# Attention backward for one query: the stores of the last head but one, moved to chosen DMA engines

## The chip, the cores and the metric

The kernel runs on one core of one Trainium2 chip. The metric is the device time of one execution in microseconds (us), from the first to the last instruction; the kernel before has a median of 1286.99 us over three runs (1286.27 to 1288.67). The core has five instruction streams: TensorE (PE, with its weight load PEld), VectorE (DVE), ScalarE (ACT), GpSimd (POOL) and SyncE (SP). Data moves between HBM and SBUF through 16 DMA engines, which all queues share. GpSimd and SyncE each issue transfers to a queue of their own.

## The reference

The forward pass is attention with one query per head; the outputs are the result and the gradients of q, k and v.

```python
B, H, Sq, Sk, D = 2, 32, 1, 8192, 128          # bf16

def _fwd_reference(q, k, v):
    scale = q.shape[-1] ** -0.5
    scores = jnp.einsum("bhqd,bhkd->bhqk", q, k) * scale
    p = _softmax(scores, axis=-1)
    return jnp.einsum("bhqk,bhkd->bhqd", p, v)

def reference(q, k, v, grad_out):
    _out, _vjp = jax.vjp(_fwd_reference, q, k, v)
    return (_out, *_vjp(grad_out))             # out, dq, dk, dv
```

There are 64 heads. For each, K and V (2 MB each) are read and dK and dV (2 MB each) are written: dV is the outer product of p and grad_out, and dK that of the gradient of the scores and q. That makes 268 MB in and 268 MB out.

## The kernel before

A head's K or V is one tile of 128 partitions x 64 rows x 128 values; each partition holds 16 KB that are contiguous in HBM too. Heads are loaded six ahead, on SyncE. The scores come out of TensorE after transposes, and VectorE writes the outer products over the tile that held K or V (`outer`, four calls a tile), which is then stored.

```python
NTILE = 12
FIRST = 6
SPREAD = range(5, 64, 9)
...
    load_eng = nc.sync
    store_eng = nc.gpsimd
...
    def by_rows(eng, dst, src, rows):

        p = 0
        for m in rows:
            pin(eng.dma_start(out=dst[p : p + m], in_=src[p : p + m], max_dma_last_dim=NT * D))
            p += m
```

Just after the first load, six rows of q are read by GpSimd, after its cursor over the DMA engines has been set back; the other rows are read by SyncE:

```python
        r0 = FIRST if w == 0 else 0
        if r0:
            pin(store_eng.inc_swdge_sem([], [], mode="reset_dge_cursor"))
            pin(
                store_eng.dma_start(
                    out=qd_nat[:r0, w, :], in_=rows[:r0], max_dma_last_dim=D
                )
            )
        pin(load_eng.dma_start(out=qd_nat[r0:BH, w, :], in_=rows[r0:BH]))
```

How a store is issued, at the end of `outer` (w is 1 for dV and 0 for dK; `ends` is the list of chunks after which something is stored: the whole tile, or for the last head each of four chunks):

```python
        if c + 1 in ends:
            at = ends.index(c + 1)
            b0, b1 = (ends[at - 1] if at else 0) * CH, (c + 1) * CH
            dst = (dv_v if w else dk_v)[i]
            if w == 0 and i in SPREAD:
                by_rows(store_eng, dst, h.tile[w], (P - 2, 2))
            else:
                eng = load_eng if len(ends) > 1 else store_eng
                pin(eng.dma_start(out=dst[:, b0:b1, :], in_=h.tile[w][:, b0:b1, :]))
```

So all stores of heads 0 to 62 are GpSimd's, one transfer of 128 rows of 16 KB each; at every ninth head from the fifth (the last is head 59) dK goes as 126 rows and 2 rows. The eight chunks of head 63 (512 KB each) are SyncE's. After the loop two small outputs of 64 rows of 256 bytes follow on SyncE:

```python
    for w, (src, dst) in enumerate(((dqT, out_1), (oT, out_0))):
        ...
        load_eng.dma_start(out=dst.rearrange("b h s d -> (b h s) d"), in_=nat[:BH, 0, :])
```

Of the kernel before, what the change touches and what calls it, by code (L numbers as in the profile page):

```python
# [20 lines left out]
SPREAD = range(5, 64, 9)  # L21
# [3 lines left out]
def kernel(  # L25
# [12 lines left out]
    B, H, Sq, D = q.shape  # L38
    Sk = k.shape[2]
    P = nc.NUM_PARTITIONS  # L40
    assert Sq == 1 and D == P
    BH = B * H
    assert BH <= P
    NT = Sk // P
# [5 lines left out]
    load_eng = nc.sync  # L50
    store_eng = nc.gpsimd
    pin = tc.keep_in_program_order
# [30 lines left out]
    def by_rows(eng, dst, src, rows):  # L83

        p = 0
        for m in rows:
            pin(eng.dma_start(out=dst[p : p + m], in_=src[p : p + m], max_dma_last_dim=NT * D))
            p += m

    def load(i, w, pieces=(NCH,)):  # L90
        h = heads[i]
        t = kvp.tile([P, NT, D], BF16, tag=f"kv{slot_of(i, w)}", name="kvt")
        h.tile[w] = t
        src = (v_v if w else k_v)[i]
        c = 0
        for m in pieces:
            n0, n1 = c * CH, (c + m) * CH
            pin(load_eng.dma_start(out=t[:, n0:n1, :], in_=src[:, n0:n1, :]))  # L98
            c += m
# [4 lines left out]
    for w, a in enumerate((q, grad_out)):  # L104
        rows = a.rearrange("b h s d -> (b h s) d")
        r0 = FIRST if w == 0 else 0
        if r0:
# [3 lines left out]
                    out=qd_nat[:r0, w, :], in_=rows[:r0], max_dma_last_dim=D  # L111
# [276 lines left out]
    def outer(i, w, c, ends):  # L388

        h = heads[i]  # L390
        n0 = c * CH
        shape = [P, CH, D // 2, 2]
        pin(
            nc.vector.tensor_tensor(  # L394
                out=h.tile[w][:, n0 : n0 + CH, :].rearrange("p n (e t) -> p n e t", t=2),
                in0=h.qb[w][:]
                .rearrange("p (e t) -> p e t", t=2)
                .unsqueeze(1)
                .to_broadcast(shape),
                in1=h.pair[w][:, n0 : n0 + CH, :].unsqueeze(2).to_broadcast(shape),  # L400
                op=ALU.mult,
            )
        )
        if c + 1 in ends:
            at = ends.index(c + 1)
            b0, b1 = (ends[at - 1] if at else 0) * CH, (c + 1) * CH
            dst = (dv_v if w else dk_v)[i]
            if w == 0 and i in SPREAD:
                by_rows(store_eng, dst, h.tile[w], (P - 2, 2))
            else:  # L410
                eng = load_eng if len(ends) > 1 else store_eng
                pin(eng.dma_start(out=dst[:, b0:b1, :], in_=h.tile[w][:, b0:b1, :]))  # L412
# [10 lines left out]
    for g in range(SL * BH + O0 + NCH + 4 - SL):  # L423
# [15 lines left out]
        if x := within(O1):  # L439
            outer(x[0], 1, x[1], last if x[0] == BH - 1 else whole)  # L440
        if x := within(O0):
            outer(x[0], 0, x[1], last if x[0] == BH - 1 else whole)
        ev = None
        if g < SL * BH:
            i, r = divmod(g, SL)
# [74 lines left out]
```

## Time and profile before

| what | before |
|---|---|
| median of three runs | 1286.99 us |
| TensorE, weight load, VectorE, ScalarE, GpSimd busy | 88%, 67%, 73%, 76%, 6% |
| SyncE's queue: share of 16 DMA engines | 49.8% |
| GpSimd's queue: share of 16 DMA engines | 48.7% |
| instruction fetch on the DMA engines | 0.7% |
| 2 MB stores on GpSimd | 119, median 66.9 us from issue to landing |
| 512 KB stores on SyncE | 8, median 24.0 us from issue to landing |
| small outputs on SyncE | 2, median 23.9 us from issue to landing |

The profile names a group of instructions by its line in the kernel, its engine and its tiles, written as output <- input. A transfer has an issue (an instruction on GpSimd or SyncE) and a landing (the moment at which its completion count is full). In the slices, the span is cut into 40 equal parts of 32.2 us; a digit is a busy share in tenths. The view of stretches gives the same for any stretch of time, with the mean busy share of the 16 DMA engines and the rate in GB/s at the end of each line.

### The profile page before, as it was taken

What the parts mean: (1) busy time and instruction counts of PE and PEld (TensorE: products, weight loads), DVE (VectorE), ACT (ScalarE), POOL (GpSimd) and SP (SyncE); (2) the same over time, 40 slices, a digit from 0 to 9 for tenths busy, and PEclk for the clock granted to TensorE, in tenths of its full rate; (3) what the DMA queues carried; (4) which work ended last, traced back from release to release, by engine and by line L of the source; (5) the groups of instructions that cost most, each with busy time, mean ns of one, the idle gap of its engine ahead of it and who ended that gap; (6) DMA issues with size and microseconds to landing.
All of it is one profiled execution on the core that took longest, in us unless ns stands there. A gap on an engine that the chain in (4) does not pass through costs nothing.

```text
span 1286.9 us, 42575 instructions
## 1 busy us (share of the span) xinstructions
PE 1131.8 (88%) x19268; PEld 860.1 (67%) x19268; DVE 935.9 (73%) x2122; ACT 975.2 (76%) x641; POOL 75.1 (6%) x142
## 2 busy tenths in 40 slices
PE   6999999988899988989899988889898988988880
PEld 5777777766677666766666766667666666766650
DVE  2888888777687777767776876777767777777781
ACT  6888888877788777867777877778777777777750
POOL 0000000000000000000000000000000000000000
PEclk9999999999899999989899998999999999999985
DMA  9999999999999999999999999999999999999995
GB/s 388 424 425 427 427 427 427 426 427 428 428 426 427 428 427 426 416 429 427 427 427 429 427 427 427 427 424 424 426 427 428 426 427 424 427 428 428 424 392 216
DMA packets 39986, 539.68 MB, mean 419 GB/s; under 512 B 5116, under 2 KB 5116, under 8 KB 6396
## 3 DMA queue, kind: packets, MB, share of 16 engines
q1 hardware_dynamic: 20172, 272.70, 49.8%
q0 software_dynamic: 19632, 264.25, 48.7%
q8 instruction: 150, 2.46, 0.7%
q14 instruction: 32, 0.26, 0.0%
HBM read 268.47 MB, written 268.47 MB: 417 GB/s over the span
## 4 chain that ended last, share of the span: by engine, by line
DMA 38%; PE 26%; another core or an unknown queue 19%; DVE 10%; issue 4%; ACT 1%; SPq 1%; POOL 0%; POOLq 0%; DVEq 0%; ACTq 0%
DMA kvt<-in_v_dram 29%; PE tp L184 11%; PE acc L339 6%; DVE kvt L394 6%; DMA kvt<-in_k_dram 5%; DMA out_dram<-kvt 4%; PE dpw L195 3%; PE sw L195 3%; DVE sel L362 2%; ACT ev L186 1%; PE dpw L282 1%; SPq L98 1%; DVE sel L356 1%; DMA qd_nat<-in_q_dram 1%
## 5 line engine op out<-in xcount | busy, mean ns | idle before, releaser
L186 ACT COPY ev<-tp 128x2048 bf16<-128x2048 bf16 x512 | 954.4, 1865 | 266.1 <-PE tp L184 254.4
L184 PE MATMUL tp<-ident_bf,kvt 128*128 128x128 bf16 x8192 | 559.9, 223 | 91.6 <-DMA kvt<-in_v_dram 71.6
L394 DVE TENSOR_TENSOR kvt<-qb,pair 128x2048 bf16<-128x2048 bf16 x512 | 621.4, 1214 | 0.3
L184 PEld LDWEIGHTS <-kvt 128*128 128x128 bf16 x8192 | 490.5, 101 | 98.3 <-DMA kvt<-in_v_dram 75.1
L195 PEld LDWEIGHTS <-ev 128*128 128x128 bf16 x8192 | 243.1, 96 | 210.0 <-issue 152.5
L339 PE MATMUL acc<-kvt,dS_pad 128*64 128x512 bf16 x1024 | 169.2, 413 | 0.8 <-DVE dqT L379 0.8
L339 PE MATMUL acc<-kvt,E_pad 128*64 128x512 bf16 x1024 | 161.0, 395 | 0.0
L195 PE MATMUL dpw<-qdT,ev 128*128 128x1 bf16 x4096 | 140.8, 164 | 17.7 <-DVE qb L177 16.9
L362 DVE SCALAR_TENSOR_TENSOR sel<-acc,diag,sel 128x128 f32<-128x128 f32 x384 | 134.7, 351 | 13.6
L195 PE MATMUL sw<-qdT,ev 128*128 128x1 bf16 x4096 | 142.0, 164 | 1.2 <-ACT ev L186 1.2
L412 POOL DMA_DIRECT2D out_dram<-kvt x119 | 63.7, 536 | 1087.6 <-DVE kvt L394 922.1
L207 DVE TENSOR_REDUCE mp<-sw 128x1 f32<-128x64 f32 x64 | 14.4, 224 | 151.8 <-PE sw L195 151.8
L339 PEld LDWEIGHTS <-dS_pad 128*64 128x64 bf16 x1024 | 37.7, 111 | 24.7 <-issue 5.9
L247 DVE CAST E_pad<-E_f 128x64 bf16<-128x64 f32 x64 | 12.5, 195 | 55.4 <-ACT E_f L238 55.4
L339 PEld LDWEIGHTS <-E_pad 128*64 128x64 bf16 x1024 | 36.5, 109 | 21.4 <-issue 0.9
L376 PE MATMUL acc<-ones,sel 128*128 128x1 f32 x256 | 43.6, 239 | 6.2 <-DVE sel L362 6.2
L282 PE MATMUL dpw<-ld,ones 128*128 128x1 f32 x256 | 46.3, 250 | 0.1
L253 DVE CUSTOM_DVE_ANT_0 junk<-E_f,dpw 128x64 bf16<-128x64 f32 x64 | 14.1, 221 | 43.7 <-PE dpw L195 43.7
L376 PEld LDWEIGHTS acc<-ones,sel 128*128 128x128 f32 x256 | 39.3, 194 | 7.3 <-DVE sel L362 7.3
L356 DVE TENSOR_SCALAR sel<-acc,diag 128x128 f32<-128x128 f32 x128 | 44.1, 344 | 0.0
L177 DVE CAST qb<-dpw 128x128 bf16<-128x128 f32 x128 | 35.5, 277 | 6.2 <-PE dpw L168 6.2
L282 PEld LDWEIGHTS dpw<-ld,ones 128*128 128x128 f32 x256 | 38.2, 189 | 0.5 <-DVE ld L253 0.5
(44 smaller groups left out, 313.2 us busy)
## 6 DMA issues: line engine op xcount, KB each, us to landing
out_dram<-kvt POOLq DMA_DIRECT2D x119, 2048.0 KB, 66.9
kvt<-in_v_dram SPq DMA_DIRECT2D x64, 2048.0 KB, 20.9
kvt<-in_k_dram SPq DMA_DIRECT2D x63, 2048.0 KB, 20.9
out_dram<-kvt POOLq DMA_DIRECT2D x7, 2016.0 KB, 70.3
out_dram<-kvt SPq DMA_DIRECT2D x8, 512.0 KB, 24.0
kvt<-in_k_dram SPq DMA_DIRECT2D x2, 512.0 KB, 4.7
kvt<-in_k_dram SPq DMA_DIRECT2D x1, 1024.0 KB, 7.3
out_dram<-kvt POOLq DMA_DIRECT2D x7, 32.0 KB, 69.7
```

The source lines that it names most:

```text
L177: pin(nc.vector.tensor_copy(out=h.qb[w][:], in_=h.qbp))
L184: pin(nc.tensor.transpose(tp[:, t, :], src[:, c * CH + t, :], ident_bf[:]))
L186: pin(nc.scalar.copy(out=ev[:], in_=tp[:]))
L195: nc.tensor.matmul(dst[:, c * CH + t : c * CH + t + 1], lhsT=ev[:, t, :], rhs=qdT[:, w, i : i + 1], start=True, stop=True,)
L207: pin(nc.vector.reduce_max(out=h.mp[:], in_=h.s, axis=AX.X))
L282: nc.tensor.matmul(out, lhsT=ones[:].to_broadcast([P, P]), rhs=col, start=True, stop=True)
L339: nc.tensor.matmul(h.acc[w][g : g + CW, :], lhsT=wts[:, n0 : n0 + CW], rhs=rows[:, n0 : n0 + QT, :].rearrange("p n d -> p (n d)"), start=( ...
L356: nc.vector.tensor_scalar(out=h.sel[:], in0=block, scalar1=diag[:, 0:1], scalar2=None, op0=ALU.mult)
L362: nc.vector.scalar_tensor_tensor(out=h.sel[:], in0=block, scalar=diag[:, b : b + 1], in1=h.sel[:], op0=ALU.mult, op1=ALU.add,)
L376: nc.tensor.matmul(h.acc[w][:, 0:1], lhsT=h.sel[:], rhs=ones[:], start=True, stop=True)
L394: nc.vector.tensor_tensor(out=h.tile[w][:, n0 : n0 + CH, :].rearrange("p n (e t) -> p n e t", t=2), in0=h.qb[w][:] .rearrange("p (e t) -> ...
L412: pin(eng.dma_start(out=dst[:, b0:b1, :], in_=h.tile[w][:, b0:b1, :]))
```

## The change

The two stores of head 62 no longer go as two transfers of 128 rows each on GpSimd's queue. dV of head 62 is cut into two transfers on GpSimd and three on SyncE, dK of head 62 into three on SyncE, with numbers of rows that are meant to lead most of the data to DMA engines 14, 15 and 0 to 3 (dV) and 0 to 3 (dK). It is for engines that have finished their share while others still have stores to write. Everything else, the chunks of head 63 included, is as before.

```diff
+    def narrow(dst, src):
+
+        m = 6 * 19
+
+        def eighths(ap, h):
+
+            parts = ap[P - 1 : P].rearrange("p (e h n) d -> p h e (n d)", e=8, h=2)
+            return parts[:, h]
+
+        pin(store_eng.dma_start(out=eighths(dst, 0), in_=eighths(src, 0)))
+        pin(store_eng.dma_start(out=dst[:m], in_=src[:m], max_dma_last_dim=NT * D))
+        for r in (slice(m, P - 1, 2), slice(m + 1, P - 1, 2)):
+            pin(load_eng.dma_start(out=dst[r], in_=src[r], max_dma_last_dim=NT * D))
+        pin(load_eng.dma_start(out=eighths(dst, 1), in_=eighths(src, 1)))
+
@@
             dst = (dv_v if w else dk_v)[i]
-            if w == 0 and i in SPREAD:
+            if i == BH - 2 and w == 1:
+                narrow(dst, h.tile[w])
+            elif i == BH - 2:
+                by_rows(load_eng, dst, h.tile[w], (76, 48, 4))
+            elif w == 0 and i in SPREAD:
                 by_rows(store_eng, dst, h.tile[w], (P - 2, 2))
```

The row that is left over in dV (the last of 128) goes as two times eight pieces of 1 KB, one half on each queue. On GpSimd the pieces stand ahead of the 114 rows.

## The prediction

> **What bounds the kernel now.** I read the slices of the page first, because the kernel moves 537 MB and does little with it.
>
> ```profile
> DMA  9999999999999999999999999999999999999995
> GB/s 388 424 425 427 427 427 427 426 427 428 428 426 427 428 427 426 416 429 427 427 427 429 427 427 427 427 424 424 426 427 428 426 427 424 427 428 428 424 392 216
> ```
>
> The 16 DMA engines are busy from the first slice to the last but one, at about 427 GB/s. No compute engine is so full (TensorE, the busiest, 88%). Only the last slice falls to 216 GB/s, so that is where a change of stores alone can win. Next the stretches of the end; the last two columns are the mean busy share of the 16 DMA engines and GB/s.
>
> ```profile
> core 0: us, PE busy (x) PEld busy (x) DVE busy (x) ACT busy (x) POOL busy (x), PEclk, DMA share, GB/s
> 1243.00:1260.00 17.00, 8.57 (x37) 3.97 (x34) 14.86 (x32) 0.00 (x0) 0.53 (x1) 0.53 0.98 409
> 1260.00:1273.00 13.00, 0.00 (x0) 0.00 (x0) 0.00 (x0) 0.00 (x0) 0.00 (x0) 0.50 0.60 252
> 1273.00:1281.00 8.00, 0.00 (x0) 0.00 (x0) 0.00 (x0) 0.00 (x0) 0.00 (x0) 0.50 0.42 173
> 1281.00:1287.00 6.00, 0.00 (x0) 0.00 (x0) 0.00 (x0) 0.00 (x0) 0.00 (x0) 0.50 0.05 19
> ```
>
> After 1260 nothing computes, yet the program lasts 26.9 us more, with 9 to 10 of 16 DMA engines working, then 7, then one. The bytes still to come are 13 x 252 + 8 x 173 + 6 x 19 = 4,774 KB. All sixteen engines at 420 GB/s (an estimate from the slices above) would need 11.4 us for them and stop near 1271. So up to some 13 us are lost to imbalance between engines. The chain of waits does not show it: its last entries end near 1259, with the last instruction that computes. Who issues what at the end, from the timelines of GpSimd and SyncE:
>
> ```profile
> 1224.94 0.53 POOL L412 DMA_DIRECT2D out_dram<-kvt  x1 [10.92 <-DVE kvt L394]
> 1233.65 0.53 POOL L412 DMA_DIRECT2D out_dram<-kvt  x1 [8.19 <-DVE kvt L394]
> 1243.38 0.53 POOL L412 DMA_DIRECT2D out_dram<-kvt  x1 [9.19 <-DVE ld L253]
> ...
> 1245.80 11.98 SPq L412 DMA_DIRECT2D out_dram<-kvt  x8
> 1259.23 4.90 SPq L489 DMA_DIRECT2D out_dram<-nat  x2
> ```
>
> The first three are dk of head 61, dv of head 62 and dk of head 62 (2 MB each, GpSimd's queue); then head 63 in eight chunks of 512 KB and the two small outputs, on SyncE's queue. The trace also keeps the sixteen moments at which a store's completion count rose, one for each DMA engine. Sorted, in us:
>
> ```
> dk 61   1231.9 1235.3 1236.8 1237.1 1237.7 1241.4 1244.0 | 1254.1 1254.4 | 1263.4 1263.4 1263.6 1264.6 1264.7 1265.2 1269.2
> dk 62   1249.8 1249.8 1249.9 1250.3 1250.9 1251.7 1254.9 | 1266.7 1267.4 | 1275.6 1275.7 1275.8 1276.8 1276.9 1277.4 1281.5
> chunk 8 1260.8 1260.8 1261.1 1261.2 1261.3 1261.9 1264.2 | 1273.3 1274.2 | 1280.5 1280.5 1280.7 1281.4 1281.5 1282.0 1285.2
> ```
>
> The same pattern three times: seven engines early, two in the middle, seven late, one of these last by 3 us. The late ones have whole stores of GpSimd's queue ahead of them that the early ones finished 25 us before.
>
> **Which engine is which.** The trace does not number them. At head 59 the kernel's spread store gives engines 4 and 5 one row in place of 8. There one engine of the early group gets through in under 4 us, when 9 rows would take 5.5, and comes out 8 us ahead of all others; one late engine moves up into the middle pair. If these are 4 and 5, six early ones are left, and eight (one middle, seven late). The change names just six engines, 14, 15 and 0 to 3, and 6 to 13 are just eight. I take it so: an inference, and the one that all rests on.
>
> **What the Trainium skill says.** The page "DMA: Bandwidth & Descriptors", section "Why a DMA increments its semaphore by 16 and not by 1", says that a transfer runs on the largest k up to 16 that divides its slowest dimension. On SyncE's queue these are the k lowest-numbered engines; on GpSimd's, k consecutive ones from a rotating cursor[...]. The trace of before uses k = 16 at the end and shows the sixteen counts, but not the choice for other shapes. Section "Queues, rings and completion order" says that each DMA engine takes its queues in turn, packet by packet, and one queue in ring order. This the trace bears out: a 16 KB packet takes 0.611 us net and a 4 KB one 0.155, so eight of each in turn make 6.13 us, and on late engines chunk after chunk lands 6.1 us apart (1255.5, 1261.6, 1267.7 on one) while the big stores last, then 1.24 us apart.
>
> **The change, part by part.** Compute and loads stay as they are, in instructions and order; the last load is issued at 1213. Only the 256 rows (16 KB each) of head 62 move.
>
> - dv of 62, before 8 rows per engine. Now eight 1 KB pieces on GpSimd, which use 6 to 13 and push the cursor from 6 (set by the first small load) to 14. Then 114 = 6 x 19 rows on 14, 15, 0, 1, 2, 3: 19 each. SyncE takes 7 rows (engines 0 to 6) and 6 rows (0 to 5), one each, and the other half row.
> - dk of 62 goes to SyncE as 76 = 4 x 19 rows on 0 to 3 (19 each), 48 = 16 x 3 (3 each), 4 rows (1 each on 0 to 3).
>
> Rows of head 62 per engine, before 16 everywhere: engines 0 to 3 get 19 + 2 + 23 = 44 (+28); 14 and 15 get 22 (+6); 4 and 5 get 5 (-11); 6 gets 4 (-12); 7 to 13 get 3 (-13). The rows come in 8 KB packets, as in the spread stores, where one takes 0.303 us net: 0.606 us a row.
>
> Late engines: 13 rows x 0.61 = 7.9 us less. The last data packet of before ends at 1284.8, on the last late engine: now 1276.9. The six others go from 1280.0 to 1281.6 to about 1272 to 1274, the middle pair to about 1266.
>
> Engines 0 to 3: from the end of dk 61 each has 44 rows x 0.606 = 26.7 us and chunks of 64 x 0.155 = 9.9 us, 36.6 us plus 0.2 for small outputs and counts. The counts come about 0.3 us after the data, so the six ended dk 61 at 1235.0, 1236.5, 1236.8, 1237.4, 1241.1 and 1243.7. They would now end at 1271.8, 1273.3, 1273.6, 1274.2, 1277.9 and 1280.5, if they are among 0 to 3. Engines 14 and 15 do 38 row-lengths in 23.4 us and end by 1267 at the latest.
>
> Which four of the six are 0 to 3 I can't read. The latest is among them with chance 4/6, slightly less if the author gave the larger share to the quicker ones. From last data to the end of the program before took 1286.9 - 1284.8 = 2.1 us. Cases: the latest among them, 1280.5 + 2.1 = 1282.6; otherwise 1277.9 + 2.1 = 1280.0; at best the late group sets it, 1276.9 + 2.1 = 1279.0. Weighted some 0.6, 0.35 and 0.05, this is 1281.5; I say 1281, a gain of 6 us or 0.5%.
>
> **A new wait that I think is hidden.** SyncE's transfers rotate over eight completion counters, and a transfer waits for the one eight before it. Before, the second small output shows it: its issue at 1263.7 follows the last landing of chunk 2 at 1263.6. Now six transfers stand ahead of the chunks, so chunks 6, 7 and 8 wait for the three parts of dk 62. On engines 0 to 3 these share with dv and end at 1260 to 1268. The late six then still have some three to six chunks of 1.24 us in their rings, so a chunk issued by 1268 should arrive just in time; this could cost 0 to 2 us.
>
> **Rivals.**
>
> - *Wrong engines.* Were one of 0 to 3 a late engine, it would get 28 x 0.606 = 17 us on top of 1281 and the program would end near 1299. For it: no number is in the trace. Against it: the groups come out as six and eight, and the change is cut to that. Chance 5%.
> - *Overfilled receivers, or the counter wait.* If 0 to 3 become the new late group with more than I count, or chunks 6 to 8 starve the rings, the gain shrinks: 1284 to 1288. For it: one early engine is 7 us behind its fellows and gets the same 28 rows. Chance 20%.
> - *Balanced end.* If the receivers are the four quickest and packets mix well, 1276 to 1279. The bytes alone allow 1271.4 + 2.1 = 1273.5. Chance 20%.
> - *Hidden anyway.* If compute set the end, nothing would change. Against it: the last compute is at 1259, 27 us before the end. Under 2%.
>
> **Range and chances.** The three cases span 1279 to 1283; a starved ring adds 2, a better mix takes 2, and the three runs of before differ by 2.4 us. That makes 1277 to 1286. Two per cent is 25.7 us, twice what perfect balance could give, so faster by over 2% is as good as out; slower by over 2% would need engines even worse chosen than in the first rival.
>
> **What would show it.** In the changed profile: stretches from 1260 to 1273 with a DMA share well over 0.60 and GB/s near 350; 2 MB stores of GpSimd fewer by two; the median time to landing of the chunks no longer at 24 us; the last counts of chunk 8 held by engines that were early, at 1278 to 1281, with the late ones down by 7 to 8 us. I would be wrong if the late group still ended at 1285, if the share after 1273 stayed low with one or two engines beyond 1283 (overfilled), or if chunks 6 to 8 were issued after 1270.

## The result and the profile after

The changed kernel takes 1299.38 us (median of four runs, 1298.96 to 1305.31) where before takes 1287.83 in the same comparison: a ratio of 1.0101, 95% interval 1.0069 to 1.0133. It is 11.5 us slower; the prediction was 6 us faster. The run in the profile is the longest of the four, with a span of 1303.5 us. The slices of its page, to be read against the two lines of before:

```profile
DMA  9999999999999999999999999999999999999983
GB/s 388 423 428 429 424 428 427 428 428 426 428 426 428 427 427 420 420 428 427 428 427 424 424 429 427 427 427 423 428 428 426 427 423 426 427 426 428 411 288 126
```

Up to the fourth last slice the two kernels are alike, then after falls behind, and in the last but one the rate falls to 288 GB/s (before 392) with the DMA engines still shown at 8. The stretches of the end say it more sharply; the last two columns are again DMA share and GB/s.

```profile
core 0: us, PE busy (x) PEld busy (x) DVE busy (x) ACT busy (x) POOL busy (x), PEclk, DMA share, GB/s
...
1243.00:1260.00 17.00, 9.99 (x82) 4.62 (x79) 16.41 (x32) 1.96 (x3) 0.00 (x0) 0.67 0.89 303
1260.00:1273.00 13.00, 0.90 (x3) 0.63 (x3) 1.34 (x6) 0.00 (x0) 0.00 (x0) 0.50 0.83 263
1273.00:1281.00 8.00, 0.00 (x0) 0.00 (x0) 0.00 (x0) 0.00 (x0) 0.00 (x0) 0.50 0.39 147
1281.00:1287.00 6.00, 0.00 (x0) 0.00 (x0) 0.00 (x0) 0.00 (x0) 0.00 (x0) 0.50 0.75 286
1287.00:1295.00 8.00, 0.00 (x0) 0.00 (x0) 0.00 (x0) 0.00 (x0) 0.00 (x0) 0.50 0.18 64
1295.00:1303.50 8.50, 0.00 (x0) 0.00 (x0) 0.00 (x0) 0.00 (x0) 0.00 (x0) 0.50 0.05 20
```

From 1260 to 1273 the share did rise, from 0.60 to 0.83, as the change intends. The bytes did not: 263 GB/s in place of 252. Before, a rate of 252 at a share of 0.60 is 420 per full share; here it is 263 / 0.83 = 317. So the engines that were given work are busy, but their packets take longer on the mean. At the end a share of 0.05 is one engine: it alone holds the program for the last 8 us.

GpSimd and SyncE at the end, from their timelines:

```profile
1226.67 0.53 POOL L431 DMA_DIRECT2D out_dram<-kvt  x1 [12.08 <-DVE kvt L409]
1234.64 0.53 POOL L99 DMA_DIRECT2D out_dram<-kvt  x1 [7.44 <-DVE kvt L409]
1239.52 1.03 POOL L100 DMA_DIRECT2D out_dram<-kvt  x1 [4.34 <-DMA out_dram<-kvt]
```

```profile
1234.06 2.28 SPq L102 DMA_DIRECT2D out_dram<-kvt  x2
1236.38 1.27 SPq L103 DMA_DIRECT2D out_dram<-kvt  x1
1246.28 6.44 SPq L87 DMA_DIRECT2D out_dram<-kvt  x3
1252.82 32.33 SPq L431 DMA_DIRECT2D out_dram<-kvt  x8
1285.31 2.56 SPq L508 DMA_DIRECT2D out_dram<-nat  x2
```

L99 is the transfer of eight 1 KB pieces, L100 the 114 rows, L102 and L103 SyncE's parts of dv, L87 the three parts of dk. The eight chunks of head 63, issued within 12.0 us before, now take 32.3: the last ones wait for the counters of the dk parts, the last of them until 1285. In the stretch with a share of 0.39 most engines have nothing to do: they have worked off what was issued, and chunk 6 waits for the first part of dk, whose last count comes at 1281.0. The moments at which the count of the first small output rose, which is issued right behind chunk 8 (the row that the prediction calls chunk 8 is of this transfer too):

```
before  1260.8 ... 1264.2 (7) | 1273.3 1274.2 | 1280.5 ... 1282.0 (6) 1285.2
after   1287.6 ... 1288.9 (14) | 1294.1 | 1302.2
```

The trace also keeps every packet. Mean time of one by stretch, in ns; q0 is GpSimd's queue, q1 SyncE's. Undisturbed (the medians throughout) a packet of 16, 8 and 4 KB takes 611, 309 and 159 ns:

```
                     q0 16 KB   q0 8 KB   q1 8 KB   q1 4 KB
before 1243-1260        619       309        -         162
after  1243-1260        696       419       436        207
before 1260-1273        611        -         -         159
after  1260-1273        741       418       482        198
```

In each group of after, 55% to 84% of the packets are still within 5% of the undisturbed time. Of the others some take over twice as long, one of 16 KB as much as 2501 ns. What makes them do so is the question of the experiments. As one number for it I take the **lost packet time**: what all packets after 1243 took beyond the undisturbed times, summed over sixteen engines. It is 4.2 us before and 97.6 after. It says how much packets waited in all, not how much later the program ends.

### The profile page after: what moved, and what is told of

Its sections match the earlier page's. It is cut to its first block, busy times and chain, and to the rows that moved or that the text cites. A ratio compares the mean times of both kernels' runs of the same rounds, so it can differ in the third digit from the quotient of the medians.

```text
span 1303.5 us, 42583 instructions
## 1 busy us (share of the span) xinstructions
PE 1136.2 (87%) x19268; PEld 862.7 (66%) x19268; DVE 936.3 (72%) x2122; ACT 975.1 (75%) x641; POOL 75.7 (6%) x142
## 4 chain that ended last, share of the span: by engine, by line
DMA 38%; another core or an unknown queue 28%; PE 17%; DVE 7%; issue 4%; ACT 2%; SPq 1%; POOL 0%; POOLq 0%; DVEq 0%; ACTq 0%
DMA kvt<-in_v_dram 18%; DMA kvt<-in_k_dram 16%; PE tp L199 8%; PE acc L354 4%; DVE kvt L409 4%; DMA out_dram<-kvt 3%; PE dpw L210 2%; PE sw L210 2%; ACT ev L201 2%; DVE sel L377 1%; SPq L113 1%; DMA qd_nat<-in_q_dram 1%; PE dpw L297 0%; DVE sel L371 0%
```

## The experiments

Two theories at the start. **Wrong engines**: the rows went to engines that were late anyway. **Ports**: it matters less which engine takes a row than how the rows of a store lie in SBUF. For the second the Trainium skill gives the means. "DMA: Bandwidth & Descriptors", section "The descriptor swizzle", says that in a transfer to 128 partitions each DMA engine serves the eight partitions of one SBUF port of its own. "SBUF — State Buffer", section "Door 1: The DMA port swizzle (why `[64,N]` ≈ `[32,N]`)", says that partitions 0 to 63 reach only 8 of the 16 ports and partitions 0 to 15 only 4, with 196 GB/s measured at 1 MiB for the 64 against 328 for all 128 partitions. If this holds for stores, 128 rows never make two engines meet, and other cuts may.

**Which engine is late: marks.** dk of head 62 on GpSimd, cut so that small transfers of two rows ("marks") go to consecutive engines, whose landing tells early or late. Rows per engine stay within two of before.

```diff
+            if w == 0 and i == BH - 2:
+                marked(dst, h.tile[w], ((112, None), (2, 4096), (2, 2048), (2, 1024), (2, 512), (2, 256), (6, None)))   # m1
+                # m2: (112, None), (10, None), (2, 2048), (2, 1024), (2, 512)
+                # m3: (112, None), (11, None), (2, 2048), (3, 1024)
```

> The kernel before, with dk of head 62 still 8 rows on every DMA engine, but cut so that five pairs of engines carry a row each in packets of a size of their own: 6 and 7 in 4 KB, 8 and 9 in 2 KB, 10 and 11 in 1 KB, 12 and 13 in 512 B, 14 and 15 in 256 B. The moment at which a size shows in GpSimd's queue says when that engine has worked off its stores. Time within 3 us of before by every theory. By my prediction's reading 6 to 13 are the late and middle engines (marks from 1266 on, up to 1282) and 14 and 15 early (marks just after issue, by 1264). If the last engine is one of 0 to 3, as the changed kernel's counts say, one of 6 to 15 more than I thought is early.

> As the marks on 6 to 15, for 0 and 1 (2 KB), 2 and 3 (1 KB), 4 and 5 (512 B). Time within 3 us of before. By my prediction's reading all of 0 to 3 show just after issue (1246 to 1256). If one of 0 to 3 is the engine that ends last, one of these four marks comes at 1275 to 1283 and the other three early.

> As before, marks shifted by one: 1 and 2 in 2 KB, 3 to 5 in 1 KB. With the pairs of the other marked kernel it names the late one of 0 to 3: a late 2 KB mark means 1 or 2, none means 0 or 3. Time within 3 us of before.

Measured, in single runs: 1294.29, 1293.1 and 1292.28 us (before in the same comparison 1288.15). All marks arrived in packets of 4 KB, so their own sizes do not tell them apart. First packets of the marks: m1 three at 1254.6, 1260.7 and 1265.8 and seven from 1278.2 to 1286; m2 two at 1254.3 and 1255.4, four from 1277.6 to 1285.4; m3 two at 1254.7 and 1256.2, three from 1278.7 to 1284.4. m2 and m3 were meant to mark engines that I took for early, and found most of them late. This fits if the plain transfers of 10 and 11 rows ahead of them did not move GpSimd's cursor, so that all marks began at engine 6.

The traces hold more than that. An engine without a row of a mark shows four small packets in its place: of 8 bytes for a mark cut at 2048, of 16, 32 and 64 bytes for 1024, 512 and 256 (56 packets for a mark of two rows, which is 14 engines, and 52 for the one of three). An early engine whose small packets are missing has the mark itself. In m2, six early engines show 20, 20 and 24 of the three sizes: one early engine has a row of the first pair, one of the second, none of the third. In m1, the five earliest engines show 16, 20, 20 and 16 of the last four sizes, so one of them has the second pair and one the fifth; a sixth engine has the first pair (its mark stands at 1260.7, its 8 bytes at 1262.1). m3 agrees. If the marks began at 6, then one of 6 and 7, one of 8 and 9 and one of 14 and 15 are early, and the other four of the seven early engines lie in 0 to 5. The numbers are inferred; the counts are in the traces.

There was a by-product: with the same rows on each engine, within two, the kernel became 4 to 6 us slower.

**Each half of the change alone.** dk as in the change with dv in one piece, and the reverse:

```diff
-            if i == BH - 2 and w == 1:
-                narrow(dst, h.tile[w])
-            elif i == BH - 2:
+            if i == BH - 2 and w == 0:      # e1: dk alone.  e2: w == 1, narrow, dv alone
                 by_rows(load_eng, dst, h.tile[w], (76, 48, 4))
```

> Only dk of head 62 is cut, 76, 48 and 4 rows on SyncE, mostly on 0 to 3; dv stays one GpSimd store. If one of 0 to 3 is late: 15 rows more on it, 9 us, about 1297. If none is: late engines lose 5 rows, 3 us, about 1285. A wait of SyncE for a completion counter would show as chunks issued after 1265 with no engine that has more to do, and 1287 or more.

> Only dv of head 62 is narrowed; dk of head 62 stays one GpSimd store on all 16 engines. If the loss comes from an engine among 0 to 3 that already ended last: it gets 19 + 2 - 8 = 13 rows more, 13 x 0.606 = 7.9 us, so 1287.8 + 8 = 1296. If the loss comes from SyncE's wait on the counters of the long dk transfers: none of those are here, so no loss, 1281 to 1288.

Measured: dk alone 1293.07 us, ratio 1.004 (1.0025 to 1.0055); dv alone 1299.24, ratio 1.0086 (1.0064 to 1.0108). Each costs; dv alone costs nearly all. Lost packet time 73.0 and 49.2 us.

dk alone also shows the counter wait by itself, in SyncE's timeline:

```profile
1243.10 5.66 SPq L87 DMA_DIRECT2D out_dram<-kvt  x3
1248.86 30.55 SPq L429 DMA_DIRECT2D out_dram<-kvt  x8
```

The chunks take 30.6 us to issue, nearly as in the full change. Yet the engine that ends last landed its chunks 1.24 us apart without a gap, from 1279.7 to 1288.4: it always had work. So the wait, though much longer than I had thought, did not set the end here. What did: the 76 rows, by the rule for k that the prediction cites from the Trainium skill on the four lowest engines, landed at 1263.2, 1265.3, 1265.7 and 1275.6. One of these four is not an early engine.

**The placement of the 114 rows.** dv of head 62 only, wholly on GpSimd, the cursor set back first, and the 114 rows led to three sets of six engines:

```diff
+            if i == BH - 2 and w == 1:
+                pin(store_eng.inc_swdge_sem([], [], mode="reset_dge_cursor"))
+                by_rows(store_eng, dst, h.tile[w], (14, 114))   # v1: 114 rows on 14, 15, 0 to 3
+                # v2: (6, 114, 8), on 6 to 11.  v3: (114, 14), on 0 to 5
```

> dv of head 62 alone is cut, on GpSimd, behind a reset of its cursor: 14 rows (one each on 0 to 13), then 114 rows, which then lie on 14, 15 and 0 to 3, as the change meant. If the changed kernel lost because its eight 1 KB pieces did not move the cursor and the 114 rows went to 6 to 11, this is better than dv alone as the change has it (1299): late engines lose 7 of 16 rows, 4.3 us, so 1283 to 1285, or about 1291 if one of 14 and 15 is late itself. If the pieces did move it, this is the same placement and 1299 again.

> As the run with 14, 15 and 0 to 3, but the 114 rows are put on 6 to 11 (six rows before them on 0 to 5, eight after them). If the pieces did not move the cursor, this repeats dv alone as the change has it: 1297 to 1301. If they did, 6 to 11 are late engines by my prediction's reading and this is worse than 1299 or equal only by accident.

> The 114 rows on 0 to 5, 14 rows on 6 to 15 and 0 to 3. If late engines all lie in 6 to 15, as the marks say once plain transfers of 10 and 11 rows are taken not to move the cursor, late engines lose 7 rows: 1287.8 - 4.3 = 1283.5. If one of 0 to 3 is late, as a long dk transfer on 0 to 3 in the changed kernel says, it gets 12 rows more: about 1295.

Measured: v1 1297.24 us, ratio 1.007 (1.0055 to 1.0085); v2 1298.12, 1.0076 (1.006 to 1.0093); v3 1292.65, 1.004 (1.0025 to 1.0055). Three sets, all slower. v2 has the picture of dv alone: four engines far behind the rest, the first small output counted at 1290.2, 1291.4, 1292.6 and 1295.9 against 1287.8, 1291.5, 1293.6 and 1294.7. Four late engines are also what the marks give for 6 to 11. So by these signs the change's 114 rows went to 6 to 11, not to 14, 15 and 0 to 3. In the changed kernel itself one engine carries a 1 KB piece (at 1282.5) and after it 38 packets of 8 KB, which are 19 rows; that could not be if the pieces went to 6 to 13 and the rows to 14 and on.

**The change as it was meant.** v1's dv together with dk in three parts on SyncE.

```diff
+            if i == BH - 2 and w == 1:
+                pin(store_eng.inc_swdge_sem([], [], mode="reset_dge_cursor"))
+                by_rows(store_eng, dst, h.tile[w], (14, 114))
+            elif i == BH - 2:
+                by_rows(load_eng, dst, h.tile[w], (76, 48, 4))
```

> The change as it was meant: dv of head 62 with 114 rows surely on 14, 15 and 0 to 3, dk on 0 to 3 through SyncE. By my prediction's rows per engine: 1281, since only the place of the 114 rows was wrong. If rows keep needing the port of their partition, moving them to other DMA engines frees nothing and adds collisions: at least as slow as each half alone (1297 and 1293), 1295 to 1303.

Measured: 1303.72 us (1296.57 to 1310.91), ratio 1.0096 (1.0059 to 1.0133). With the rows where they were meant to be it is no better than the change. This alone does not part the two theories, since two of these six engines (one of 14 and 15, one of 0 to 3) are not early either. But the first part of dk landed at 1280.1, 1281.0 and 1281.9 on the three quicker engines and at 1289.1 on the fourth, where the prediction had all parts by 1268: the quick ones are late too. Lost packet time: 113.5 us.

**Equal rows, other cut.** Now nothing is moved between engines. Both stores of head 62 in two halves, on GpSimd: of 64 rows (p1), and as a control of 128 rows with half the columns (p2). Each engine gets eight times 16 KB per store in all of these.

```diff
+            if i == BH - 2:
+                for r in (slice(0, 64), slice(64, P)):      # p2: halves of the columns instead
+                    pin(store_eng.dma_start(out=dst[r], in_=h.tile[w][r]))
```

> Both stores of head 62 cut into two transfers of 64 rows each on GpSimd. Every DMA engine still moves 8 rows a store, so by counting rows per engine nothing changes: 1288. If what counts is that a row leaves SBUF through the port of its partition, 64 rows reach only half the ports, two engines share each, and packets of these stores show twice their 0.61 us where both are at it: 2 to 10 us slower, 1290 to 1298, with the rate of 1243 to 1260 well under the 409 GB/s of before. If cutting alone costs, this and the column halves are slower alike.

> The control for the row halves: the same stores cut into two transfers of all 128 rows and half the columns each, so as many transfers, 8 KB packets, and all ports in each. By rows per engine and by ports alike: 1286 to 1290, packets at 0.31 us. If cutting alone costs: as slow as the row halves.

Measured: row halves 1299.64 us, ratio 1.0072 (1.0048 to 1.0097); column halves 1287.69, ratio 0.9995 (0.9984 to 1.0005). The stretches of row halves, then of column halves:

```profile
1243.00:1260.00 17.00, 8.53 (x38) 3.69 (x36) 15.13 (x32) 0.00 (x0) 1.07 (x2) 0.57 0.96 332
1260.00:1273.00 13.00, 0.00 (x0) 0.00 (x0) 0.00 (x0) 0.00 (x0) 0.00 (x0) 0.50 0.82 265
```

```profile
1243.00:1260.00 17.00, 7.92 (x42) 3.66 (x39) 15.29 (x32) 0.00 (x0) 1.05 (x2) 0.62 0.99 406
1260.00:1273.00 13.00, 0.00 (x0) 0.00 (x0) 0.00 (x0) 0.00 (x0) 0.00 (x0) 0.50 0.60 251
```

Row halves have the changed kernel's signature (0.82 and 265, against 0.83 and 263), column halves that of before (0.60 and 251, against 0.60 and 252). Two transfers in place of one cost nothing; the lines between rows do. The size fits as well: if two stores of 2 MB run at half rate, each loses 2.10 MB / 427 GB/s = 4.9 us, together 9.8; a ratio of 1.0072 is 9.3 us.

**Ports or places in HBM.** The row halves change both which ports of SBUF are read together and which places in HBM are written together. Two kernels part them: sixteen rows at a time, which narrows the ports to four and keeps the order in HBM; and the row halves with the first half written to the even rows of the output and the second to the odd ones, which leaves SBUF as in p1. In this last one dv and dk of head 62 therefore lie in another order than the reference has them.

```diff
-                for r in (slice(0, 64), slice(64, P)):
-                    pin(store_eng.dma_start(out=dst[r], in_=h.tile[w][r]))
+                for r in (slice(16 * e, 16 * e + 16) for e in range(8)):                            # q16
+                for r, z in ((slice(0, 64), slice(0, P, 2)), (slice(64, P), slice(1, P, 2))):      # q2
+                    pin(store_eng.dma_start(out=dst[z], in_=h.tile[w][r]))
```

> Both stores of head 62 as eight transfers of 16 rows each, one row for each DMA engine. If the ports of SBUF set it (16 partitions reach 4 of 16 ports by the Trainium skill, 64 reach 8): packets of up to four times 611 ns, 2.4 us, and more loss than the halves' 11.5 us, up to some 29 us (each 2 MB store at a quarter of the rate, 3 x 4.9 us more, twice), less where the engines drift apart over several transfers: 1300 to 1318. If it were only that a cut store disturbs the order of the engines: as the halves, 1297 to 1301, packets not above 1250 ns.

> Both stores of head 62 as two transfers of 64 rows each, but the rows of the first half go to the even rows of the output and those of the second to the odd ones, so that the places in HBM are 32 KB apart in place of 16 KB (the output of this head has its rows in another order). If the ports of SBUF set it: as the halves, 1297 to 1301, 90th percentile of 16 KB packets near 1244 ns. If the places in HBM did: another time, near 1288 if the wider spread frees them.

Measured: eighths 1294.61 us, ratio 1.0053 (1.0038 to 1.0068); halves with other places in HBM 1299.03, ratio 1.0083 (1.0067 to 1.01). The 16 KB packets of GpSimd's queue from 1233 to 1290, by their time in ns:

```
                        under 650   650-1100   1100-1350   1350-2200   over 2200
before                     574         25          6           1           1
row halves (p1)            386        113         97          13           1
halves, other HBM (q2)     387        102         92          15           4
row eighths (q16)          412         90         39          31          30
```

The other places in HBM change nothing: the same time and the same heap at 1100 to 1350, twice 611. Eighths bring packets that the halves have hardly any of: 30 over 2200, the longest 3508; four times 611 is 2444. Both speak for the ports. The lost packet time of the eighths is the highest of all, 144.1 us (halves 108.8, column halves 5.5). On the time of the eighths I was wrong: 1294.6, below the 1300 to 1318 for ports and below the halves too. GpSimd's timeline shows one reason:

```profile
1243.90 0.96 POOL L410 DMA_DIRECT2D out_dram<-kvt  x2 [6.55 <-DMA out_dram<-kvt]
1248.80 0.48 POOL L410 DMA_DIRECT2D out_dram<-kvt  x1 [3.94 <-DMA out_dram<-kvt]
1255.31 0.48 POOL L410 DMA_DIRECT2D out_dram<-kvt  x1 [6.02 <-DMA out_dram<-kvt]
1262.53 0.48 POOL L410 DMA_DIRECT2D out_dram<-kvt  x1 [6.74 <-DMA out_dram<-kvt]
```

The sixteen transfers wait for landings of earlier ones and are issued from 1234 to 1280, so few of them run together with others of their kind. That this is all of the difference was not tested.

**Is it only the end?** In the steady run half of the packets are loads, which write SBUF. I thought that the reading side might have room there, because the 126-row stores of every ninth head show packets near the undisturbed 309 ns. So: row halves for both stores of head 40 (`if i == 40` in place of `i == BH - 2`).

> Both stores of head 40 as two transfers of 64 rows each, in the middle of the run where loads still run, in place of head 62 (which cost 11.5 us there). If the two halves of the DMA engines collide only when all engines read SBUF: the time stays at 1288 to 1290, and 16 KB packets around head 40 keep about 611 to 650 ns. If a cut store costs the same everywhere: 1297 to 1300, and many packets above 1100 ns for the some 13 us that the two stores take longer.

Measured: 1299.09 us, ratio 1.008 (1.0055 to 1.0105). My idea fell: a cut store costs the same there. The stretches of this kernel, then of before:

```profile
800.00:840.00 40.00, 33.89 (x598) 25.96 (x599) 28.09 (x65) 29.43 (x21) 2.42 (x4) 1.00 1.01 424
840.00:880.00 40.00, 33.23 (x555) 25.13 (x552) 26.54 (x62) 28.35 (x19) 2.77 (x5) 0.93 1.00 381
880.00:920.00 40.00, 31.64 (x450) 23.25 (x449) 21.66 (x49) 22.59 (x16) 2.12 (x4) 0.80 1.00 393
```

```profile
840.00:880.00 40.00, 35.05 (x567) 26.31 (x568) 27.19 (x64) 28.60 (x20) 2.15 (x4) 0.91 1.01 424
880.00:920.00 40.00, 37.45 (x659) 28.64 (x656) 32.60 (x74) 33.83 (x22) 2.12 (x4) 1.00 1.01 424
```

The DMA share is full and the rate still falls by 43 and 31 GB/s, which over 40 us each is 3.0 MB or 7.0 us. Stores alone are slow in it: from 840 to 920 the 16 KB packets take 699 ns on GpSimd's queue and 615 on SyncE's, which carries the loads (before 623 and 614). So here packets that read SBUF were slowed, and those that write it were not.

**Uneven stores in the steady run.** Three kernels on the stores that the kernel before already cuts: without the last one, at head 59 (p8); p8 with dv of head 52 as 114 and 14 rows on engines 0 to 5 (b1); and none at all (s0).

```diff
-SPREAD = range(5, 64, 9)
+SPREAD = range(5, 59, 9)     # p8, and b1 with the lines of v3 for i == 52.   s0: SPREAD = ()
```

> An attempt to beat the kernel before: its last uneven store (126 and 2 rows, head 59) goes as one store of 128 rows. Engines 4 and 5 get 7 rows more (4.3 us) at a moment when they are not the last; the others get one row less and no collisions in that store, which in the kernel before show as packets of 0.395 in place of 0.309 us between 1230 and 1243. Collision theory: 1285 to 1288. If 4 or 5 sets the end: 1290 to 1292.

> The uneven store of head 59 left out (worth 1284.2 alone), and dv of head 52 as 114 and 14 rows with the cursor set back, so that engines 0 to 5 get 19 rows plus 2 or 3 of the other 14 and the rest less, while loads run. If rows can be moved between DMA engines while loads run: the late engines lose some 7 rows, 4 us, and the time is 1280 to 1282. If the data stay bound to their ports of SBUF there too, nothing is won: 1284 to 1290.

> No uneven store at any head; all stores of heads 0 to 62 are 128 rows on GpSimd's queue. If the uneven stores cost only where loads have ended: the late engines are no longer relieved at heads 5 to 50 (6 stores; each gives engines 4 and 5 one row in place of eight and the others more), so the lag between engines changes, but the time stays within 1282 to 1288. If each uneven store costs some us wherever it is: faster than 1282. If they pay as meant: slower than 1286.

Measured: p8 **1284.22 us**, ratio 0.996 (0.9944 to 0.9976), which beats both kernels. b1 1291.79, ratio 1.0029 (1.0016 to 1.0042): 7.6 us above p8, where rows moved at no cost to early engines would have given 1280 to 1282. From 1050 to 1090 and from 1090 to 1120 it moves 400 and 413 GB/s where before moves 424 and 427; that is 1.4 MB or 3.2 us. The rest was not traced, and by the marks two of 0 to 5 are not early. s0 1304.02, ratio 1.0128 (1.0111 to 1.0144).

What head 59 costs, in one stretch of before and then of p8:

```profile
1230.00:1243.00 13.00, 12.48 (x223) 9.20 (x219) 10.63 (x22) 10.62 (x8) 0.53 (x1) 1.00 0.95 362
```

```profile
1230.00:1243.00 13.00, 11.24 (x175) 8.24 (x173) 8.96 (x20) 8.72 (x5) 0.53 (x1) 0.87 0.96 408
```

The same share, 362 against 408 GB/s; 46 x 13 = 0.6 MB or 1.4 us at 427 of the 4 us are seen here. The 8 KB packets of the cut store take 395 ns there, while those of the 126-row store of head 50 (1017 to 1077) take 314. And s0 shows that uneven stores do pay. Its DMA issues and a late stretch:

```profile
kvt<-in_v_dram SPq DMA_DIRECT2D x64, 2048.0 KB, 49.3
kvt<-in_k_dram SPq DMA_DIRECT2D x63, 2048.0 KB, 49.4
```

```profile
1243.00:1260.00 17.00, 15.88 (x248) 11.94 (x248) 11.56 (x30) 12.35 (x10) 1.06 (x2) 0.90 0.58 245
```

A load takes 49 us to land in place of about 20, since one engine is some 23 us behind the fifteen others (a store counted at 1227.7 to 1232.5 on fifteen and at 1255.4 on one), and with it come all tiles late. Six stores of 126 rows mend this and bring 1304.0 - 1284.2 = 19.8 us. Rows can thus be taken off an engine; but of the cuts tried only that into 126 was nearly free of slow packets; those with 114, 112, 76 or 64 were not (lost packet time after 1243: v1 81.7 us, m1 85.8, dk alone 73.0, row halves 108.8).

## Why the prediction was wrong

- **What bounds the kernel**: right. The end is a matter of imbalance between DMA engines, and compute is beside it. Packets alternate between the queues, and the steady slices are those of before.
- **"0.606 us a row"**, the price in every sum: this is the step that failed first. It was taken from 128-row and 126-row stores and carried over to cuts of 114, 76 and 48 rows, where a packet of 8 KB takes 418 to 482 ns on the mean in place of 309. The packets of uncut stores beside them pay too: those of 16 KB, 696 and 741 ns in place of 619 and 611. That the cut between rows makes packets dear is shown by row halves against column halves: 9.3 us against none, with the same rows on each engine. That engines meet at SBUF's ports is strongly supported: twice the time for 64 rows, up to four times and more for 16, stores slow and loads beside them not, and no difference from the one other order in HBM that was tried. The trace names no port, so I do not call it seen.
- **"Late engines: 13 rows x 0.61 = 7.9 us less"** fell with it. GpSimd's last rows of head 62 land at 1301.1, where everything of the late group was to be done by 1276.9. Moving rows to other engines does not help if their cut makes packets wait, or if the engine is late itself.
- **"eight 1 KB pieces on GpSimd, which use 6 to 13 and push the cursor from 6 to 14"**: wrong. The section "Why a DMA increments its semaphore by 16 and not by 1" of the Trainium skill's "DMA: Bandwidth & Descriptors" gives the rule for k and the cursor; the rows behaved as though the piece transfer had left the cursor at 6 (dv alone is like v2, and one engine carries both a piece and rows). This sent 19 rows each to engines that were late already.
- **"14, 15 and 0 to 3"** as the early six, "the one that all rests on": wrong. One of 0 to 3 ends 10 us after the three others in dk alone, and by the marks only one of 14 and 15 is early, while one of 6 and 7 and one of 8 and 9 are. So of the six named, four are early, if the marks began at engine 6; that is inferred. The row read as chunk 8 was that of the first small output; chunk 8 itself has counts from 1260.1 to 1285.1, and nothing rests on the difference.
- **The rival "wrong engines"** named 1299, the time that came, and it was part of the cause. It is not all of it, as the engine that ends last in the profiled run shows. It works through its 38 packets from 1282.9 to 1300.5, 30 of them at 309 ns and all together only 0.9 us above, but it begins them late. The last counts of the stores ahead of them, which the change leaves alone, and of head 62:

  ```
            dk 60    dv 61    dk 61    head 62
  before   1257.0   1263.1   1269.2    1281.5
  after    1270.3   1276.4   1282.5    1301.1
  ```

  Of the 16.6 us between the two spans (1286.9 and 1303.5), 13.3 were there before the first moved row on this engine. Its eight rows of dk 60 alone took 11.1 us (6.1 before). If it is one of 6 to 11, the change puts at most four rows of head 62 on SyncE's queue ahead of it, 8 packets of 309 ns or 2.5 us. So slow packets of stores that were not cut make up most of the 13.3 us. This holds for this run, the longest of the four; the split in the other three is not known. A rival with the right number is not thereby the right one.
- **The counter wait**, "0 to 2 us": the chunks were issued until 1285 and not by 1268. In dk alone, with the same wait, the last engine never ran dry. In the full change the last engine has no gap from 1282.9 on, so there too other engines stood idle and not the one that set the end.
- **What would show it**: I had set the DMA share from 1260 to 1273 "well over 0.60" as a sign of success, together with a rate near 350. The share came (0.83), the rate did not (263). Only the pair of numbers tells work from waiting.
- The loss is not a sum of parts: dk alone +4.8 us, dv alone +11.1, both +11.5 (each against the before measured with it). How much of it is slow packets and how much misplaced rows is known only for the one run above. Of the three placements v3 is 5.5 us below v2, and v1, the one meant, is like v2 (0.9 us apart, the intervals overlap); none of the three comes down to the time of before.

## What to carry to other kernels

Before rows are moved between DMA engines, look at how they lie in SBUF: in these runs a store of all 128 partitions, or a slice of its columns, kept its packet times, and a cut between rows doubled the time of many packets, also of other stores. To judge such a change, read the DMA share and the GB/s of a stretch together; here a share that rose while the rate stayed was packets waiting. Uneven stores can still pay where one engine lags far behind, if their cut is one whose packets keep their time, and they are better left out where the run is about to end.

## What the runs showed of the hardware that I had not expected

- A store cut into two times 64 rows: a heap of 16 KB packets at 1100 to 1350 ns in place of 611; cut into 16 rows, 30 packets of 602 over 2200. Loads beside such stores stay at 615; uncut stores beside the cuts of the change rise from 611 to 741.
- One pair of cut stores costs some 9 to 11 us, at head 40 as at head 62, although each engine moves the same bytes.
- Without uneven stores one of the sixteen engines falls some 23 us behind, and the time grows to 1304.0 us; six stores of 126 rows bring 1284.2, a seventh near the end takes it to 1288.2.
- SyncE issues a transfer only when the one eight before it has landed: six transfers ahead of the chunks held the issue of the last chunk back to 1285, where before it was out by 1257.8 (1245.80 + 11.98).
